# Products of a zero tile in every turn of an attention opening, and a new order at its end

## Chip, cores, metric

One core of a Trainium2 chip. The metric is the device time of one execution in microseconds; lower is better.

## The reference

Attention with a window and sinks, and two pairs of dense layers behind it:

```python
keep = (pos < n_sink) | ((rel >= 0) & (rel < window))      # n_sink 4, window 128, S = 768
a = softmax(where(keep, q @ k.T / 8, -1e9))                # B = 2, H = 8, D = 64
x = (a @ v) as [1536, 512]
h = x @ w_in;  g = max(h, 0) + alpha * min(h, 0);  y = g @ w_out       # 512 -> 2048 -> 512
h = y @ w2_in; g = h - tanh(h);                    out = g @ w2_out
```

## The kernel before

Queries and keys are divided into blocks of 128 positions: 12 units u (two batches of six blocks i), each with four pairs p of heads, so 48 pairs n = 4u + p. A pair goes through these steps, each on one engine:

- s_mm(n) (PE, lines 264 and 270): scores of the two heads of a pair, into two banks. In the opening these come from four banks "o", afterwards from "s" and "t". For the first unit the operands are the raw f32 tiles; later ones are split in a high and a low part by splits_hi (ACT, line 234) and splits_lo (DVE, line 237).
- s_max(n, a) (DVE, line 279): mask and row maximum; s_exp(n, a) (ACT, line 288): exponential and sum; norm_sum and norm (DVE, lines 294 to 303); sink_copy (DVE, line 309).
- t_mm(n) (PE, line 319): transposes into a bank "t" or "h", in turns; t_ev(n) (ACT, line 326) copies them out. sink_mm and sink_ev (PE line 341, ACT line 345) do the same for the sink columns; sink_mm(n - 1, n + 1) writes into the second score bank of pair n + 1.
- pv(n) (PE, lines 358 to 362): product with the values, line 362 for sinks; x_h (ACT, line 369) and x_l (DVE, line 374) copy a unit's sum out as a high and a low part.

The weights of the layers come as pairs of 32-bit words. A conversion makes them f32 in two ACT passes (lines 73 and 74, conv_start) and two DVE passes (lines 76 and 78, one conv_step each); load_w fetches a block of weights on SP's queue into one of two buffers, which the second DVE pass frees. split_w (ACT, line 215) and split_lo (DVE, line 220) then make high and low parts for the products, h_mm (line 389) and out_mm (line 441).

The kernel is written in the order in which each engine's queue runs it: nothing is reordered. The opening is a loop over S_LEAD = 19 turns n = 0 to 18. In turn n it issues the loads of the turn, s_mm(n + 1), t_ev(n - 2), s_max(n), s_exp(n), norm(n - 1), t_mm(n - 1), pv(n - 2), the splits of keys, and, by a table, conversions (0, 0) from turn 8 and (0, 1) from turn 12. After the loop conversion (0, 2) is started. Then 96 steps g follow, one for each block of 128 hidden units and 512 tokens, and the first 32 of them also carry the remaining pairs. Step 0 begins with t_mm(17), t_ev(17), sink_mm(17, 19) and sink_ev(17), and has s_mm(19) in the middle of its h_mm.

Of the kernel before, what the change touches and what calls it, by code (L numbers as in the profile page):

```python
# [14 lines left out]
BF16 = mybir.dt.bfloat16  # L15
# [7 lines left out]
S_LEAD = 19  # L23
CONV0 = ((0, 8), (1, 12))
# [7 lines left out]
CH = 512  # L32
# [106 lines left out]
def fast_path(tc, qk, v, vsink, limits, w1i, w1o, alpha, w2i, w2o, out, outer):  # L139
    nc = tc.nc  # L140
    keep = outer.enter_context(tc.tile_pool(name="keep", bufs=1))
    bad_i = keep.tile([1, 1], I32, name="bad_i")
    with ExitStack() as ctx:
        def pool(name, bufs=1, **kw):
            return ctx.enter_context(tc.tile_pool(name=name, bufs=bufs, **kw))
# [4 lines left out]
        gp = pool("g", 2)  # L150
# [49 lines left out]
        def conv_w(m, f):  # L200
            raw = stage[m][f % 2]
            if m == 1 and f < 3:
                wf[m, f] = ap.tile([128, 1024], F32, name="wf", tag="wx" if f == 2 else "pq", bufs=1 if f == 2 else 2)
            else:
                wf[m, f] = wp.tile([128, 1024], F32, name="wf", tag="wf", bufs=NF)
            at = m * NF + f
            yield from convert_scaled(nc, raw.rearrange("p (n t) -> p n t", t=2), wf[m, f], seen[:, at:at + 1])
# [3 lines left out]
        def split_w(m, c, f, part):  # L211
            src = wf[m, f][:, 512 * part:512 * part + 512]
            hi = wp.tile([128, 512], F32R, name=f"wh{part}", tag=f"wh{part}", bufs=2)
            lo = wp.tile([128, 512], F32R, name=f"wl{part}", tag=f"wl{part}", bufs=2)
            nc.scalar.activation(out=hi, in_=src, func=AF.Copy, scale=W_DOWN)  # L215
            whl[m, c, f, part] = (hi, lo)

        def split_lo(m, c, f, part):
            hi, lo = whl[m, c, f, part]
            nc.vector.scalar_tensor_tensor(lo, wf[m, f][:, 512 * part:512 * part + 512], W_DOWN, hi, op0=ALU.mult, op1=ALU.subtract)  # L220
# [3 lines left out]
        pq, sums, ptb, pts, vps, sks, sps, tps = {}, {}, {}, {}, {}, {}, {}, {}  # L224
        initial = [True]
# [19 lines left out]
        def ps_tile(tags):  # L245
            rot[0] += 1
            tag = tags[rot[0] % len(tags)]
            return ps.tile([128, 512], F32, name="ps_" + tag, tag=tag, bufs=4 if tag == "o" else 1)

        def geom(n):  # L250
            u, p = divmod(n, 4)
            b, i = divmod(u, NB)
            return u, p, b, i, (128 if i == 0 else 288)

        def s_mm(n):

            u, p, b, i, w = geom(n)
            for a in range(2):
                if (n, a) not in sps:
                    sps[n, a] = ps_tile(["o"] if initial[0] else ["st"[a]])  # L260
            if u == 0:
                for a in range(2):
                    t = raws[2 * u + p // 2][64 * a:64 * a + 64, p % 2]
                    nc.tensor.matmul(sps[n, a][:, :w], lhsT=t[:, 0, :], rhs=t[:, 1, :], start=True, stop=True)
                return
            at = 0 if u % 2 == 0 else K_ODD + 128
            for e, (l, r) in enumerate(((0, 0), (1, 0), (0, 1))):
                for a in range(2):
                    h = slice(64 * a, 64 * a + 64)
                    nc.tensor.matmul(sps[n, a][:, :w], lhsT=kq[l][h, p, at:at + 128], rhs=kq[r][h, p, K_EVEN:K_EVEN + w], start=e == 0, stop=e == 2)  # L270

        def s_max(n, a):
            u, p, b, i, w = geom(n)
            G, hh = 2 * u + p // 2, 2 * (p % 2) + a
            if hh == 0:
                pq[G] = ap.tile([128, 4, 288], F32, name="pq", bufs=2)
                sums[G] = ap.tile([128, 4], F32, name="sums", bufs=2)
            mask = m_zero if i == 0 else m_one if i == 1 else m_even if i % 2 == 0 else m_odd
            nc.vector.tensor_tensor_reduce(  # L279
                out=pq[G][:, hh, 0:w], in0=sps.pop((n, a))[:, :w], in1=mask[:, 0:w], scale=-0.125, scalar=BIG,  # L280
                op0=ALU.add, op1=ALU.min, accum_out=nm[:, 2 * n + a:2 * n + a + 1],
            )

        def s_exp(n, a):
            u, p, b, i, w = geom(n)
            G, hh = 2 * u + p // 2, 2 * (p % 2) + a
            e = pq[G][:, hh, 0:w]
            nc.scalar.activation(out=e, in_=e, func=AF.Exp, scale=-1.0, bias=nm[:, 2 * n + a:2 * n + a + 1], accum_out=sums[G][:, hh:hh + 1])  # L288
# [22 lines left out]
        def t_mm(n):  # L311
            u, p, b, i, w = geom(n)
            G, hh = 2 * u + p // 2, 2 * (p % 2)
            tps[n] = t = ps_tile(["t", "h"] if initial[0] else ["t"])
            cur = 0 if i % 2 == 0 else 160
            for a in range(2):
                for e, c in ((0, 160 - cur), (1, cur)):
                    if i > 0 or e == 1:
                        nc.tensor.transpose(t[:, 256 * a + 128 * e:256 * a + 128 * e + 128], pq[G][:, hh + a, c:c + 128], ident)  # L319

        def t_ev(n):
            u, p, b, i, w = geom(n)
            ptb[n] = ap.tile([128, 2, 2, 128], F32, name="pt", bufs=2)
            e0 = 1 if i == 0 else 0
            tv = tps.pop(n).rearrange("p (a e c) -> p a e c", a=2, e=2)
            nc.scalar.activation(out=ptb[n][:, :, e0:, :], in_=tv[:, :, e0:, :], func=AF.Copy)  # L326

        def has_sinks(n):
            u, p, b, i, w = geom(n)
            return p % 2 == 1 and i >= 2  # L330
# [12 lines left out]
        def sink_ev(n):  # L343
            pts[n // 2] = ap.tile([128, 128], F32, name="pts", bufs=2)
            nc.scalar.activation(out=pts[n // 2], in_=tps.pop((n, 0))[:, 384:512], func=AF.Copy)
# [142 lines left out]
        rel_i = wp.tile([128, 128], I32, name="rel_i", tag="wl0", bufs=2)  # L488
        rel = wp.tile([128, 128], F32, name="rel", tag="wh1", bufs=2)
        sink = wp.tile([128, 128], F32, name="sink", tag="wl1", bufs=2)  # L490
        nc.gpsimd.iota(rel_i, pattern=[[-1, 128]], base=0, channel_multiplier=1)
        nc.gpsimd.iota(col_i, pattern=[[1, 128]], base=0, channel_multiplier=0)
        make_identity(nc, ident)
# [26 lines left out]
        def a_loads(n):  # L520

            u, p = divmod(n, 4)
            if p == 3 and 2 <= u + 1 < NU:
                load_v(u + 1)
            if n % 2 == 0 and 6 <= n // 2 + 4 < 2 * NU:
                load_qk(n // 2 + 4)
            if n == 4 * NB + 4:
                load_vs(1)
# [19 lines left out]
        def conv_start(m, f):  # L548
            convs[m, f] = conv_w(m, f)
            next(convs[m, f])  # L550
# [5 lines left out]
        for n in range(S_LEAD):  # L556
            last = n == S_LEAD - 1
            a_loads(n)
            if n == 0:
                s_mm(0)  # L560
            if not last:
                s_mm(n + 1)
            if n >= 2:
                t_ev(n - 2)
            s_max(n, 0)
            s_max(n, 1)
            s_exp(n, 0)
            s_exp(n, 1)
            if n >= 2 and has_sinks(n - 2):
                sink_ev(n - 2)  # L570
            if n >= 1:
                norm_sum(n - 1, 0)
                norm_sum(n - 1, 1)
                norm(n - 1)
                sink_copy(n - 1)
                if not last:
                    t_mm(n - 1)
                    if has_sinks(n - 1):
                        sink_mm(n - 1, n + 1)
            if n >= 2 and not last:  # L580
                pv(n - 2)
            splits_hi(n)
            if n >= 5 and n % 4 == 1:
                x_h(n - 2)
            splits_lo(n)
            if n >= 5 and n % 4 == 2:
                x_l(n - 3)
            if n == 1:
                masks(0)
            if n == 4:  # L590
                masks(1)
            if n == 3:
                load_w(0, 1)
            for f, at in CONV0:
                if n == at:
                    conv_start(0, f)
                if at < n < at + 5:
                    conv_step(0, f)
                if n == at + 4:
                    load_w(0, f + 2)  # L600
                if n == at + 6 and f == 0:
                    split_w(0, 0, 0, 0)
                    split_lo(0, 0, 0, 0)
        initial[0] = False
        conv_start(0, len(CONV0))


        def flag():
# [36 lines left out]
        start = {t: f for f, t in enumerate(t for t in range(CONV1, CONV1 + NF + 1) if t != 2 * NF + 2)}  # L645
        for g in range(N):
            m, c, f = steps[g]
            n = S_LEAD + g
# [332 lines left out]
```

## Time and profile before

| | us |
|---|---|
| median of three runs | 668.03 (666.78 to 668.26) |
| the profiled execution | 665.62 |
| its span, first to last instruction | 663.9 |
| PE matmuls busy | 635.1 (96%) |
| DVE busy | 528.7 (80%) |
| ACT busy | 472.5 (71%) |

Busy time is that of instructions, without issues and semaphores. PE is the matmul part of TensorE, PEld its weight loads. A busy PE need not be at its peak: matmuls overlap, and the granted clock (PEclk, as a share of 2.4 GHz) has two levels.

### The profile page before, as it was taken

The numbers are of one execution on the slowest core, as the hardware profiler recorded it, in microseconds if no ns is written. First come the engines' busy times: TensorE is split into PE (matmuls) and PEld (weight loads), VectorE is DVE, ScalarE is ACT, GpSimd is POOL, SyncE is SP. The second block draws the span as 40 slices with busy tenths as digits, with TensorE's granted clock in tenths as the row PEclk, the third lists the DMA queues.
The fourth block names the chain that finished last, engine by engine and source line by source line (L and its number), as shares of the span: only waits on it lengthen the run. The fifth ranks groups of instructions, "written<-read, shape, count | busy, mean of one in ns | idle before, by whom it ended". The sixth has DMA issues, their size and how long they took to land.

```text
span 663.9 us, 9193 instructions
## 1 busy us (share of the span) xinstructions
PE 635.1 (96%) x3194; PEld 502.5 (76%) x3194; DVE 528.7 (80%) x1098; ACT 472.5 (71%) x936; POOL 1.1 (0%) x8
## 2 busy tenths in 40 slices
PE   5867999999999999999999999999999999999995
PEld 3545677777777777777888888888888888888884
DVE  7987888899576666548999978888898888888873
ACT  5877888787566565557877767777777777777763
POOL 0000000000000000000000000000000000000000
PEclk9988999999999999999999999999999999999999
DMA  5542444453010000214355500000010000100001
GB/s 157 190 147 95 144 159 173 165 202 112 3 46 17 1 16 1 77 53 170 147 190 191 190 1 1 0 1 0 1 64 0 2 0 1 63 1 1 0 1 69
DMA packets 27032, 47.36 MB, mean 71 GB/s; under 512 B 3168, under 2 KB 15456, under 8 KB 26976
## 3 DMA queue, kind: packets, MB, share of 16 engines
q1 hardware_dynamic: 26400, 46.42, 20.0%
q8 instruction: 27, 0.44, 0.3%
q10 hardware_dynamic: 576, 0.26, 0.2%
q14 instruction: 29, 0.24, 0.1%
HBM read 43.53 MB, written 3.15 MB: 70 GB/s over the span
## 4 chain that ended last, share of the span: by engine, by line
PE 82%; ACT 6%; DVE 6%; DMA 2%; issue 2%; SPq 0%; ACTq 0%; DVEq 0%
PE ps_o L441 36%; PE ps_h L389 19%; PE ps_s L389 9%; PE ps_t L389 8%; PE ps_s L270 2%; PE ps_t L319 2%; PE ps_v L358 2%; PE ps_v L362 2%; ACT wf L73 1%; PE ps_v L359 1%; DMA raw<-in_moe_w_out_dram 1%; DMA raw_qk<-in_qk_dram 1%; ACT raw L74 1%; DVE pq L279 1%; DVE wf L76 1%
## 5 line engine op out<-in xcount | busy, mean ns | idle before, releaser
L220 DVE SCALAR_TENSOR_TENSOR wl<-wf,wh 128x512 fp32r<-128x512 f32 x192 | 123.5, 683 | 44.1 <-ACT wh L215 44.1
L215 ACT ACTIVATE wh<-wf 128x512 fp32r<-128x512 f32 x192 | 110.8, 629 | 3.2 <-PE ps_o L441 3.1
L389 PE MATMUL ps_h<-x,wh 128*128 128x512 f32 x296 | 97.1, 409 | 0.3 <-DVE x L374 0.2
L441 PE MATMUL ps_o<-gh,wh 128*128 128x512 f32 x192 | 76.5, 398 | 0.0
L441 PE MATMUL ps_o<-wh,gh 128*128 128x512 f32 x192 | 74.8, 390 | 0.2 <-ACT gh L420 0.2
L441 PE MATMUL ps_o<-gh,wl 128*128 128x512 f32 x192 | 74.9, 390 | 0.0
L441 PE MATMUL ps_o<-wh,gl 128*128 128x512 f32 x192 | 74.8, 390 | 0.0
L441 PE MATMUL ps_o<-gl,wh 128*128 128x512 f32 x192 | 74.8, 390 | 0.0
L441 PE MATMUL ps_o<-wl,gh 128*128 128x512 f32 x192 | 74.7, 389 | 0.0
L288 ACT ACTIVATE pq<-pq,nm 128x288 f32<-128x288 f32 (+1 forms) x96 | 48.4, 506 | 30.3 <-DVE nm L279 29.8
L389 PEld LDWEIGHTS ps_h<-x,wh 128*128 128x128 f32 x296 | 52.5, 190 | 11.8 <-issue 2.0
L389 PE MATMUL ps_h<-x,wl 128*128 128x512 f32 x148 | 58.8, 397 | 0.3 <-DVE wl L220 0.3
L420 ACT ACTIVATE gh<-g 128x512 fp32r<-128x512 f32 x48 | 30.4, 633 | 29.6 <-DVE g L127 29.6
L326 ACT ACTIVATE pt<-ps_t 128x512 f32<-128x512 f32 (+1 forms) x39 | 21.9, 561 | 35.2 <-PE ps_t L319 35.1
L76 DVE SCALAR_TENSOR_TENSOR wf<-wf,raw 128x1024 int32<-128x1024 int32 x32 | 39.1, 1222 | 9.9 <-ACT raw L74 9.8
L441 PEld LDWEIGHTS ps_o<-gh,wh 128*128 128x128 f32 x192 | 36.0, 188 | 8.4 <-issue 1.4
L441 PEld LDWEIGHTS ps_o<-wh,gh 128*128 128x128 f32 x192 | 36.0, 188 | 8.0 <-ACT gh L420 0.6
L441 PEld LDWEIGHTS ps_o<-wh,gl 128*128 128x128 f32 x192 | 36.0, 188 | 7.9 <-DVE gl L425 0.4
L441 PEld LDWEIGHTS ps_o<-gh,wl 128*128 128x128 f32 x192 | 36.0, 188 | 7.7
L441 PEld LDWEIGHTS ps_o<-wl,gh 128*128 128x128 f32 x192 | 36.0, 188 | 7.5
L441 PEld LDWEIGHTS ps_o<-gl,wh 128*128 128x128 f32 x192 | 36.1, 188 | 7.1
L127 DVE COPY_PREDICATED g<-mask,t 128x512 f32<-128x512 int32 x48 | 36.4, 759 | 4.9
(155 smaller groups left out, 1339.4 us busy)
## 6 DMA issues: line engine op xcount, KB each, us to landing
raw<-in_moe_w_in_dram SPq DMA_DIRECT2D x32, 512.0 KB, 3.3
raw<-in_moe_w_out_dram SPq DMA_DIRECT2D x32, 512.0 KB, 4.2
raw_qk<-in_qk_dram SPq DMA_DIRECT2D x92, 64.0 KB, 3.0
vt<-in_v_dram SPq DMA_DIRECT2D x12, 256.0 KB, 3.2
out_dram<-ob SPq DMA_DIRECT2D x2, 1024.0 KB, 4.2
out_dram<-ob SPq DMA_DIRECT2D x4, 256.0 KB, 3.1
vs<-in_vsink_dram SPq DMA_DIRECT2D x2, 256.0 KB, 3.3
raw_qk<-in_qk_dram ACTq DMA_DIRECT2D x4, 64.0 KB, 2.8
```

The source lines that it names most:

```text
L76: nc.vector.scalar_tensor_tensor(di, di, 3, lw, op0=ALU.logical_shift_left, op1=ALU.bitwise_or)
L127: nc.vector.copy_predicated(g, mask.bitcast(I32), t)
L215: nc.scalar.activation(out=hi, in_=src, func=AF.Copy, scale=W_DOWN)
L220: nc.vector.scalar_tensor_tensor(lo, wf[m, f][:, 512 * part:512 * part + 512], W_DOWN, hi, op0=ALU.mult, op1=ALU.subtract)
L270: nc.tensor.matmul(sps[n, a][:, :w], lhsT=kq[l][h, p, at:at + 128], rhs=kq[r][h, p, K_EVEN:K_EVEN + w], start=e == 0, stop=e == 2)
L288: nc.scalar.activation(out=e, in_=e, func=AF.Exp, scale=-1.0, bias=nm[:, 2 * n + a:2 * n + a + 1], accum_out=sums[G][:, hh:hh + 1])
L319: nc.tensor.transpose(t[:, 256 * a + 128 * e:256 * a + 128 * e + 128], pq[G][:, hh + a, c:c + 128], ident)
L326: nc.scalar.activation(out=ptb[n][:, :, e0:, :], in_=tv[:, :, e0:, :], func=AF.Copy)
L358: nc.tensor.matmul(d, lhsT=vt[u - 1][:, h * D:(h + 1) * D], rhs=pt[:, a, 0, :], start=p == 0, stop=False)
L389: nc.tensor.matmul(h_ps[f], lhsT=l[:, w], rhs=x[:, r, kk, :], start=kk == 0 and e == 0, stop=kk == 3 and e == 2)
L420: nc.scalar.activation(out=gh, in_=mid[f], func=AF.Copy)
L441: nc.tensor.matmul(o, lhsT=l, rhs=r, start=f == 0 and e == 0, stop=f == NF - 1 and e == 2)
```

## The change

Five edits, all in the opening:

- A tile of 128 x 512 zeros in bf16 is made by POOL ahead of its other work. keep_busy(k, bank) multiplies it by itself k times into a bank; nobody reads the result.
- Nine such products stand at the start, before the first scores, in a bank "t".
- In every turn but the last, products follow s_mm(n + 1): four in turn 0, three in turn 1, eight in turn 2, two in each other. They go into the bank that t_mm(n - 1) of the same turn overwrites; that bank is now taken there, and t_mm uses it.
- load_w(0, 2) and load_w(0, 3) come one turn earlier (turns 11 and 15, not 12 and 16).
- split_w(0, 0, 0, 0) stays in turn 14, its split_lo moves from turn 14 to turn 16, and the start of conversion (0, 2) moves from behind the loop to the end of turn 16.

```diff
         def t_mm(n):
...
-            tps[n] = t = ps_tile(["t", "h"] if initial[0] else ["t"])
+            t = tps[n] if n in tps else ps_tile(["t"])
+            tps[n] = t
...
+        idle = gp.tile([128, CH], BF16, name="idle", tag="t", bufs=3)
+
+        def keep_busy(k, bank):
+            for _ in range(k):
+                nc.tensor.matmul(bank, lhsT=idle[:, 0:128], rhs=idle, start=True, stop=True)
+
+        nc.gpsimd.memset(idle, 0.0)
+        keep_busy(9, ps_tile(["t"]))
...
             if not last:
                 s_mm(n + 1)
+                tps[n - 1] = ps_tile(["t", "h"])
+                keep_busy({0: 4, 1: 3, 2: 8}.get(n, 2), tps[n - 1])
...
                     conv_step(0, f)
-                if n == at + 4:
+                if n == at + 3:
                     load_w(0, f + 2)
-                if n == at + 6 and f == 0:
-                    split_w(0, 0, 0, 0)
-                    split_lo(0, 0, 0, 0)
+            if n == S_LEAD - 5:
+                split_w(0, 0, 0, 0)
+            if n == S_LEAD - 3:
+                split_lo(0, 0, 0, 0)
+                conv_start(0, len(CONV0))
         initial[0] = False
-        conv_start(0, len(CONV0))
```

## Rows read from the trace of the kernel before

**Rows 1.** Stretches: its bounds and length, busy us (instructions) by engine, granted clock, DMA.
```profile
5.13:59.41 54.28, 41.98 (x298) 29.12 (x299) 46.04 (x187) 39.76 (x114) 0.00 (x0) 0.94 0.53 168
5.13:12.51 7.38, 4.43 (x18) 3.20 (x19) 5.54 (x31) 4.71 (x16) 0.00 (x0) 1.00 0.61 169
12.51:24.07 11.56, 11.56 (x62) 7.25 (x63) 10.85 (x52) 8.31 (x26) 0.00 (x0) 1.00 0.79 264
37.80:41.05 3.25, 3.25 (x18) 2.42 (x19) 1.84 (x8) 2.60 (x8) 0.00 (x0) 0.50 0.87 320
51.10:54.60 3.50, 3.50 (x20) 2.60 (x22) 2.61 (x11) 1.75 (x6) 0.00 (x0) 0.53 0.93 343
65.00:68.30 3.30, 3.30 (x14) 2.04 (x14) 3.20 (x11) 2.35 (x6) 0.00 (x0) 0.50 0.02 5
80.00:90.00 10.00, 10.00 (x59) 7.33 (x57) 9.61 (x20) 9.65 (x20) 0.00 (x0) 1.00 0.38 132
```

**Rows 2.** Timeline of PE: start, us, engine, line, instructions.
```profile
20.96 1.09 PE L270 MATMUL ps_o<-kq 64*128 64x288 f32 x6
...
25.85 0.66 PE L270 MATMUL ps_o<-kq 64*128 64x288 f32 x6
...
27.62 0.66 PE L270 MATMUL ps_o<-kq 64*128 64x288 f32 x6
```

**Rows 3.** Chain that ended last, in order of time: start, us, what.
```profile
64.57 2.50 PE ps_h L389 x6
...
83.19 1.39 PE ps_h L389 x6
...
86.77 2.72 PE ps_o L441 x12
```

**Rows 4.** Timeline of DVE; in brackets the idle time before, and its releaser.
```profile
21.71 0.69 DVE L374 TENSOR_TENSOR x<-ps_v,x 128x512 fp32r<-128x512 f32 x1 [0.30 <-ACT x L369]
...
29.73 1.23 DVE L76 SCALAR_TENSOR_TENSOR wf<-wf,raw 128x1024 int32<-128x1024 int32 x1 [0.78 <-ACT raw L74]
...
39.48 0.46 DVE L279 CUSTOM_DVE_ANT_0 pq<-ps_o,m_odd 128x288 f32<-128x288 f32 x1 [0.51 <-PE ps_o L270]
...
40.74 0.46 DVE L279 CUSTOM_DVE_ANT_0 pq<-ps_o,m_odd 128x288 f32<-128x288 f32 x1 [0.79 <-PE ps_o L341]
...
47.68 0.69 DVE L220 SCALAR_TENSOR_TENSOR wl<-wf,wh 128x512 fp32r<-128x512 f32 x1 [1.19 <-ACT wh L215]
...
49.43 0.45 DVE L279 CUSTOM_DVE_ANT_0 pq<-ps_o,m_odd 128x288 f32<-128x288 f32 x1
...
55.10 0.46 DVE L279 CUSTOM_DVE_ANT_0 pq<-ps_o,m_even 128x288 f32<-128x288 f32 x1 [1.29 <-PE ps_o L270]
```

**Rows 5.** Timeline of PE, instructions behind an idle time.
```profile
5.13 1.72 PE L264 MATMUL ps_o<-raw_qk 64*128 64x128 f32 x8 [5.13 <-DMA raw_qk<-in_qk_dram]
...
30.23 0.45 PE L358 MATMUL ps_v<-pt,vt 128*64 128x128 f32 x4 [1.37 <-ACT pt L326]
...
36.25 0.63 PE L319 MATMUL ps_h<-ident,pq 128*128 128x128 f32 x4 [1.75 <-DVE pq L303]
...
51.10 0.91 PE L319 MATMUL ps_h<-ident,pq 128*128 128x128 f32 x4 [3.64 <-DVE pq L303]
...
63.91 0.40 PE L270 MATMUL ps_s<-kq 64*128 64x288 f32 x1 [1.72 <-ACT pts L345]
```

**Rows 6.** Timeline of ACT, 58 to 68 us.
```profile
58.99 0.60 ACT L369 ACTIVATE x<-ps_v 128x512 fp32r<-128x512 f32 x1 [1.46 <-PE ps_v L362]
...
61.00 1.13 ACT L73 ACTIVATE wf<-raw 128x1024 f32<-128x1024 f32 x1
...
63.11 0.58 ACT L326 ACTIVATE pt<-ps_t 128x512 f32<-128x512 f32 x1
...
67.09 0.60 ACT L396 ACTIVATE t<-ps_h 128x512 f32<-128x512 f32 x1 [0.73 <-PE ps_h L389]
```

**Rows 7.** Timeline of POOL, start of the kernel.
```profile
1.20 0.28 POOL masks.py:197 MEMSET ident<- 128x128 f32 x1
```

## Prediction, made before the changed kernel ran

> **What bounds the kernel now.** I read the granted clock and the busy time by stretch first, then the chain that ended last, then what each engine waited for in the first 70 us. From about 80 us on, TensorE is the bound: a stretch of 10.00 us has 10.00 us of matmul [rows 1], and the chain of waits there is mostly products of the two layers [rows 3]. Nothing in the change touches that part, so I take it that an opening that ends earlier by some time brings the end forward by that time.
>
> The opening (turns n = 0 to 18, up to about 61 us) is another matter. From 5.13 to 59.41, PE is busy 41.98 of 54.28 us, DVE 46.04, ACT 39.76 [rows 1]. PE's figure is swollen by a low clock. The page prints a granted clock of 1.00 up to 37.80, but the same six score products take 1.09 us at 20.96 and 0.66 us at 25.85 [rows 2]: PE ran at the lower level, 1.2 GHz, until between these two. It fell back at 37.80, 51.10 and 65.00, each time for some 3.3 us [rows 1]. Ahead of the falls PE had sat idle 1.75 us (until 36.25), 3.64 us (until 51.10) and 1.72 us (until 63.91); no fall came after an idle of 1.37 us [rows 5]. The Trainium skill, "TensorE: Matmul & The Clock Gate", Part 1, says that the throttled level is the default and activity releases it, and warns that recorded clock events can be unreliable; both agree with these rows.
>
> The engine that sets the opening's pace is DVE. Where it does sit idle is to be seen one by one [rows 4]: 0.30 us at 21.71, 0.78 at 29.73, 0.51 and 0.79 at 39.48 and 40.74, 1.19 at 47.68, 1.29 at 55.10. A gain in the opening has to come out of these, or out of the ACT queue behind 61.00, where DVE and PE wait together.
>
> **The change part by part.**
>
> *The zero products.* Each is 512 columns wide. I cost one by the 512-column products here: 2.50/6 = 0.42 us at the low clock, 2.72/12 = 0.23 us at the full one [rows 3]. They are in bf16, which the trace lacks; those rows are the bound above, and 0 (PE idle anyway) the one below. There are 9 before turn 0, then 4, 3 and 8, then 2 in each of turns 3 to 17: 54, or 12.3 us at the full clock. In a turn they stand behind s_mm(n+1) and ahead of t_mm(n-1). Their bank is the one that t_ev(n-3) empties, and pv(n-3), a turn earlier on PE, has waited for that already: no new wait. Queued behind them are t_mm, sink_mm and pv; t_mm waits for DVE's norm in any case, so they are free where PE is early.
>
> *The start.* POOL first clears the zero tile. Its 128x128 f32 memset takes 0.28 us [rows 7]; this tile has twice the bytes and four times the elements, so 0.56 to 1.12 us; begun where POOL's first work of the kernel begins, 0.4 us before that memset's 1.20, it is ready at 1.4 to 1.95. Nine products at 0.42 end at 5.2 to 5.75, while the first score products now start at 5.13 [rows 5]. Loss 0.1 to 0.6 us; I take 0.3, nearer the lower end since a rise within the nine shortens them. POOL's iotas come later too, but DVE does nothing with them that is urgent before the limits land. PE then works without a break: nine products (3.8 us), the eight of s_mm(0) and s_mm(1) (1.72 us, [rows 5]) and four more (1.7 us), to about 9 us. So I expect the rise there and not near 24.
>
> *5 to 31 us.* With the full clock, PE is no longer late for x_h: the 0.30 us of DVE at 21.71 goes. ACT waited there too; ahead of L74 it then runs about 1 us earlier, and most of the 0.78 at 29.73 goes. Gain 1.0 of 1.08; below, 0, if ACT is held by DVE in the old places.
>
> *37.8 to 41 us.* The idle of 1.75 us before 36.25 gets two products (0.45), leaving 1.3, less than the 1.37 that was followed by no fall. If the clock stays, s_mm(13) ends by 38.75 and the 0.51 goes; two products push t_mm(11) and sink_mm back by 0.45, so of the 0.79 only a little goes. s_max(13, 1) starts near 40.1 instead of 40.74 [rows 4]: gain 0.6 (0 if the clock falls, 1.1 if the products hide).
>
> *split_lo moved from turn 14 to 16.* DVE now waits 1.19 us, until 47.68, for ACT's split_w, and then takes about 0.6 for split_lo; both leave turn 14, and L78 follows x_l directly. s_max(15) starts at 47.6 instead of 49.43 [rows 4]: 1.8 us earlier. In turn 16 the 0.61 falls where DVE idles 1.29 us [rows 4], so it stays hidden there; without that cover the gain would be 1.2. The long PE idle before 51.10 shortens by the same 1.8, and by 0.45 of products, to about 1.4.
>
> *Turns 16 and 17.* Now t_mm(14) starts 1.67 us behind s_max(15) (51.10 to 49.43, [rows 4, 5]); then at 49.3. A PE turn without idle is 27.62 - 25.85 = 1.77 us [rows 2], and pv(13) has about 0.7 of sink products, so s_mm(17) ends at 51.7, two products at 52.15, t_mm(15) and sink_mm at 53.0. DVE, through s_max(16), norm(15), sink_copy and the moved split_lo, comes to s_max(17, 0) at 52.5 instead of 55.10: 2.6 us earlier, of which 1.8 are counted and 0.8 are new, nearly all of it the low clock from 51.10 on. Its second half waits for the sink_mm at 53.0; 0 if the clock falls again.
>
> *conv_start(0, 2) moved from behind turn 18 to turn 16.* On ACT it fills 61.00 to 63.11, and t_ev(17) behind it, at 63.11, empties the t bank (sink_ev behind it the s bank): PE waits 1.72 us until 63.91 [rows 5, 6]. In turn 16 it goes behind kq_hi, 52.3 to 54.5, and makes t_ev(15) and s_exp(17) late; but ACT idles 1.46 us before 58.99 [rows 6], which pays most of it. s_exp(18) then ends at 59.1 and t_ev(17) starts there: 4.0 us earlier than 63.11, of which 2.6 are counted. Gain 1.4 (bounds: 2.1 if all is hidden, 0 if pv(15) and x_h behind t_ev(15) come late).
>
> *Behind 60 us.* With no PE idle of 1.72 us the fall at 65.00 should go. Six hidden products then take 1.39 instead of 2.50 us [rows 3], but the copy out of them (67.09, [rows 6]) stands behind s_exp(19) on ACT, at 62.8: 4.3 earlier in all, 0.3 new.
>
> *The loads a turn earlier.* load_w(0, 2) and load_w(0, 3) leave when the conversions (0, 0) and (0, 1) have freed their buffers. In SP's queue they come to stand ahead of load_qk(10) and load_qk(12) instead of behind them, so those keys now wait for the conversions too. The keys are first read in turns 16 and 21, four turns or more behind their place in the queue, and conversion (0, 2) reads its weights at 52 us, so I cost both at nothing. Without that cover a late key would hold s_mm, and all of DVE behind it, for one turn (about 2 us).
>
> **Sum:** +0.3 - 1.0 - 0.6 - 1.8 - 0.8 - 1.4 - 0.3 = -5.6 us. The profiled execution took 665.62 us (span 663.9 and 1.7 around it), so 660.0 for one like it. The runs shown have a median of 668.03, 2.4 above it; from there 662.4. A measurement tells about 0.2% (1.3 us) from no change.
>
> **The rivals.**
>
> *The products hold PE back (664 to 666.0).* With 0.45 of products a PE turn of 1.77 becomes 2.2 us, and turns 10 to 17 add sink products. If the 0.45 stands on the path in all eight, 3.6 of the 5.6 go: 666.0. For it: in turns 12 and 16 my own walk has PE late. Against: 41.98 us of PE work, less about half of the low-clock stretches (11.56 + 3.25 + 3.50 and part of 4.43, [rows 1]: about -10), plus 12.3, is 44 of 54 us. The Trainium skill, same page, Part 2, says that matmuls stay in program order and only weight loads are pulled ahead. By that no transpose overtakes a zero product; were all 30 of turns 3 to 17 on the path, that is 6.8 us, 669.2.
>
> *The clock falls in spite of them (664.1).* The idles left, 1.3 and 1.4 us, lie close to the 1.72 that was followed by a fall. Then the terms 0.6, 0.8 and 0.3 go: 5.6 - 1.7 = 3.9, 664.1.
>
> *Zero products don't raise the clock (slower, 670.9).* Then 25 of them in turns 0 to 7 cost 0.42 each, 10.5 us; PE's idle of 7.38 - 4.43 = 2.95 in 5.13 to 12.51 [rows 1] hides some and 7.5 stay; the 1.0 is not won, and of the gains 4.9 are left (5.9 less 1.0): +0.3 + 7.5 - 4.9 = +2.9. It decides if the low clock lasts past about turn 6, at 0.84 us a turn. Against it: the rise near 24 came behind short real products alone [rows 1], and PE is no less occupied by zeros.
>
> *Given back later (668.0).* What comes earlier out of the opening could wait the longer behind 61 us, for weights or ACT. Against: PE is full from 80 us on [rows 1], and loads there start when a conversion frees a buffer, so they come earlier with the rest.
>
> **Chances.** Forecast 0.60 (own range 660.0 to 664.0); products on the path 0.14; falls 0.12; not raised 0.07; given back 0.07. Range 659.8 to 666.4: it takes in the second and third cases, and a gain of 8 us if the ordinary runs lose more to low clock than the profiled one did. Faster: the first three, less 0.04 for their weak ends, 0.82; same 0.10; slower 0.08.
>
> **What would show it.** Right: score products at 0.66 us by turn 3; no granted clock of 0.50 between 24 and 70 us; no DVE wait at L220 in turn 14; conversion (0, 2) on ACT before 56 us; the first s_mm into the s and t banks near 60 instead of 63.91; the first matmul of scores at 5.2 to 5.75. Wrong: t_mm waiting for PE rather than for DVE in most turns, a fall near 36 or 48 us, or scores still at 1.09 us at 15 us.

## The result and the profile after

| | before | changed |
|---|---|---|
| median, us | 667.40 (four runs, 666.58 to 668.26) | 659.89 (four runs, 659.62 to 660.14) |
| profiled execution | 665.62 | 660.14 |
| its span | 663.9 | 658.4 |

The ratio of the times is 0.9897, with an interval of 0.9879 to 0.9915: some 6.9 us faster. The forecast was 662.4 (659.8 to 666.4); the measured median lies 0.1 us above the lower end of that range. Between the two profiled executions the gain is 5.48 us, where the sum of the terms said 5.6.

The clock first. These are the windows of the changed kernel, with the columns of [rows 1]:

```profile
5.28:57.00 51.72, 44.39 (x345) 26.91 (x349) 46.39 (x189) 42.88 (x120) 0.00 (x0) 1.00 0.56 181
12.51:24.07 11.56, 10.87 (x82) 5.95 (x85) 11.21 (x53) 9.28 (x29) 0.00 (x0) 1.00 0.80 268
37.80:41.05 3.25, 3.20 (x30) 2.19 (x30) 2.66 (x12) 3.24 (x7) 0.00 (x0) 1.00 0.63 191
60.00:70.00 10.00, 8.84 (x56) 6.26 (x55) 9.04 (x21) 9.63 (x21) 0.00 (x0) 1.00 0.38 132
```

From the first scores on, no stretch of the opening has a low clock any more. PE has 44.39 us of work in it, close to the 44 that the prediction worked out, and DVE still has more, 46.39. The products and the first scores, in the timelines of POOL and PE:

```profile
0.75 0.53 POOL L498 MEMSET idle<- 128x512 bf16 x1 [0.29 <-POOLq L980]
...
1.33 4.02 PE L496 MATMUL ps_t<-idle 128*128 128x512 bf16 x9 [1.33 <-POOL idle L498]
5.28 1.14 PE L264 MATMUL ps_o<-raw_qk 64*128 64x128 f32 x8
...
13.11 0.66 PE L270 MATMUL ps_o<-kq 64*128 64x288 f32 x6
```

The nine products take 0.45 us each, and right behind them the eight products of the first scores take 1.14 us instead of 1.72 [rows 5]. So the clock rose at about 5.3 us, as the first real product began; the same six score products that took 1.09 us at 20.96 [rows 2] take 0.66 at 13.11.

Next, the places at which engines waited before, now in the timelines of DVE, of PE and of ACT:

```profile
29.30 1.23 DVE L76 SCALAR_TENSOR_TENSOR wf<-wf,raw 128x1024 int32<-128x1024 int32 x1 [1.17 <-ACT raw L74]
...
39.40 0.46 DVE L279 CUSTOM_DVE_ANT_0 pq<-ps_o,m_odd 128x288 f32<-128x288 f32 x1 [0.48 <-PE ps_o L342]
...
50.49 0.68 DVE L220 SCALAR_TENSOR_TENSOR wl<-wf,wh 128x512 fp32r<-128x512 f32 x1
51.09 0.45 DVE L279 CUSTOM_DVE_ANT_0 pq<-ps_o,m_even 128x288 f32<-128x288 f32 x1
```

```profile
29.80 0.45 PE L359 MATMUL ps_v<-pt,vt 128*64 128x128 f32 x4 [1.33 <-ACT pt L327]
...
35.73 0.72 PE L320 MATMUL ps_h<-ident,pq 128*128 128x128 f32 x4 [1.10 <-DVE pq L303]
...
47.77 0.72 PE L320 MATMUL ps_h<-ident,pq 128*128 128x128 f32 x4 [0.91 <-DVE pq L303]
...
58.56 0.40 PE L270 MATMUL ps_s<-kq 64*128 64x288 f32 x1
```

```profile
26.50 0.63 ACT L234 ACTIVATE kq<-raw_qk 128x512 fp32r<-128x512 f32 x1 [0.79 <-DMA raw_qk<-in_qk_dram]
...
50.76 1.17 ACT L73 ACTIVATE wf<-raw 128x1024 f32<-128x1024 f32 x1
...
57.54 0.59 ACT L327 ACTIVATE pt<-ps_t 128x512 f32<-128x512 f32 x1
...
61.33 0.57 ACT L397 ACTIVATE t<-ps_h 128x512 f32<-128x512 f32 x1
```

Lines of the pairs' functions and behind are one higher than before (t_mm is now L320). The reader is to see three things. The 1.19 us wait at L220 is gone (50.49, in turn 16, no idle in front), and so is the wait of 1.29 in front of s_max(17, 0). PE's idles of 1.75 and 3.64 us [rows 5] are now 1.10 and 0.91, and the 1.72 us in front of the first s_mm behind the loop are gone (58.56). And one wait has grown: DVE's 0.78 us in front of L76 [rows 4] is now 1.17, because ACT stood 0.79 us waiting for a load of keys at 26.50.

The gain, read off at the points that the prediction's steps name (each point's start, before and after, and the difference):

| point | before | after | gain so far | this step | forecast of it |
|---|---|---|---|---|---|
| first splits_lo (L237) | 7.84 | 7.61 | 0.23 | 0.2 | -0.3 |
| s_max(10, 0) | 30.87 | 30.44 | 0.43 | 0.2 | 1.0 |
| s_max(13, 1) | 40.74 | 39.40 | 1.34 | 0.9 | 0.6 |
| s_max(15, 0) | 49.43 | 46.19 | 3.24 | 1.9 | 1.8 |
| s_max(17, 0) | 55.10 | 51.09 | 4.01 | 0.8 | 0.8 |
| t_ev(17) | 63.11 | 57.54 | 5.57 | 1.6 | 1.4 |
| copy out of h (L396, now L397) | 67.09 | 61.33 | 5.76 | 0.2 | 0.3 |

I then followed the copies of the first layer's result (gh), step by step through the 96 steps. They are 5.80 us earlier from 73 to 87 us, 5.40 at 96, 5.06 at 103, 5.38 at 111, and stay between 5.3 and 5.5 nearly all the way to the end, 5.43. So 0.4 of the gain is lost once, near 83 us.

### The profile page after: what moved, and what is told of

Same layout as the page of the kernel before. It is cut to its first block, busy times and chain, and to the rows that moved or that the text cites. A ratio compares the mean times of both kernels' runs of the same rounds, so it can differ in the third digit from the quotient of the medians.

```text
span 658.4 us, 9283 instructions
## 1 busy us (share of the span) xinstructions
PE 639.4 (97%) x3243; PEld 500.0 (76%) x3248; DVE 528.2 (80%) x1098; ACT 472.0 (72%) x936; POOL 1.7 (0%) x9
## 4 chain that ended last, share of the span: by engine, by line
PE 79%; DVE 10%; ACT 5%; DMA 3%; issue 2%; SPq 0%; DVEq 0%; ACTq 0%
PE ps_o L442 36%; PE ps_h L390 19%; PE ps_s L390 9%; PE ps_t L390 8%; PE ps_s L270 2%; DVE pq L279 2%; DMA raw_qk<-in_qk_dram 1%; DMA raw<-in_moe_w_out_dram 1%; PE ps_t L320 1%; PE ps_v L359 1%; DVE wf L78 1%; PE ps_v L363 1%; DVE wf L76 1%; ACT raw L74 1%; DVE wl L220 1%
## 5 line engine op out<-in xcount | busy, mean ns | idle before, releaser
L220 DVE SCALAR_TENSOR_TENSOR wl<-wf,wh 128x512 fp32r<-128x512 f32 x192 | 123.5, 683 | 42.9 <-ACT wh L215 42.9
L442 PE MATMUL ps_o<-gh,wl 128*128 128x512 f32 x192 | 74.9, 390 | 0.0
L76 DVE SCALAR_TENSOR_TENSOR wf<-wf,raw 128x1024 int32<-128x1024 int32 x32 | 39.1, 1223 | 8.6 <-ACT raw L74 8.2
```

Of the source, the lines that this page charges most:

```text
L76: nc.vector.scalar_tensor_tensor(di, di, 3, lw, op0=ALU.logical_shift_left, op1=ALU.bitwise_or)
L442: nc.tensor.matmul(o, lhsT=l, rhs=r, start=f == 0 and e == 0, stop=f == NF - 1 and e == 2)
```

## The experiments

In each, the edit is to the changed kernel. All ratios are to the kernel before, run on the same chip as the experiment, with an interval of 95%.

### The two halves of the change

**The order without the products.** No zero tile, t_mm takes its bank itself; the loads, split_lo and the conversion stand in the new order.

```diff
-            t = tps[n] if n in tps else ps_tile(["t"])
-            tps[n] = t
+            tps[n] = t = ps_tile(["t", "h"] if initial[0] else ["t"])
...
-        nc.gpsimd.memset(idle, 0.0)
-        keep_busy(9, ps_tile(["t"]))
...
-                tps[n - 1] = ps_tile(["t", "h"])
-                keep_busy({0: 4, 1: 3, 2: 8}.get(n, 2), tps[n - 1])
```

> The new order without any zero product. Theory (about half of the gain is order, half is clock): split_lo's wait of 1.19 us and the conversion behind turn 18 are gone, about 3.3 us of the 7.5 us between the medians, so near 664 us, with granted clock 0.50 still seen near 38 and 51 us and scores at 1.09 us until past 20 us. Rival A (the order is all, low clock was hidden behind DVE and ACT): within 1 us of the changed kernel, 659.5 to 661. Rival B (the clock is all): 666 to 667.4.

Measured: 662.06 us (661.13 to 663.88), ratio 0.9935 (0.9911 to 0.9959), profiled 661.92. The order alone brings some 4.3 us, more than expected. Its timeline of PE and two windows:

```profile
36.79 0.63 PE L319 MATMUL ps_h<-ident,pq 128*128 128x128 f32 x4 [1.74 <-DVE pq L303]
...
48.53 0.70 PE L319 MATMUL ps_h<-ident,pq 128*128 128x128 f32 x4 [1.63 <-DVE pq L303]
```

```profile
36.80:40.20 3.40, 3.40 (x33) 2.59 (x35) 3.20 (x14) 2.79 (x8) 0.00 (x0) 1.00 0.95 349
49.00:52.30 3.30, 3.30 (x20) 2.40 (x18) 2.75 (x11) 1.95 (x9) 0.00 (x0) 0.50 0.92 337
```

An idle of 1.74 us was followed by no fall of the clock here, and one of 1.63 us by the only fall of this run's opening.

**The products without the order.**

```diff
-                if n == at + 3:
+                if n == at + 4:
                     load_w(0, f + 2)
-            if n == S_LEAD - 5:
-                split_w(0, 0, 0, 0)
-            if n == S_LEAD - 3:
-                split_lo(0, 0, 0, 0)
-                conv_start(0, len(CONV0))
+                if n == at + 6 and f == 0:
+                    split_w(0, 0, 0, 0)
+                    split_lo(0, 0, 0, 0)
         initial[0] = False
+        conv_start(0, len(CONV0))
```

> The old order with all 54 zero products. Theory: the clock part alone, some 4 us, so near 663.5; DVE waits 1.2 us at split_lo in turn 14 again and PE waits for the conversion behind turn 18. Rival A (order is all): 666 to 668. Rival B (clock is all): 659.5 to 661.

Measured: 665.72 us (664.97 to 666.71), ratio 0.9988 (0.9977 to 0.9998), profiled 665.68. The products alone bring some 0.8 us between runs and nothing between the profiled executions, less than the 4 us expected. Together the two bring 6.9 where the parts add up to 5.1, and 5.5 against 3.6 in the profiled executions (3.7 and -0.1). Why the whole is more than its parts shows in this run's timelines, of DVE and of PE, and its window behind them:

```profile
46.25 0.69 DVE L220 SCALAR_TENSOR_TENSOR wl<-wf,wh 128x512 fp32r<-128x512 f32 x1 [1.50 <-ACT wh L215]
...
54.79 0.46 DVE L279 CUSTOM_DVE_ANT_0 pq<-ps_o,m_even 128x288 f32<-128x288 f32 x1 [1.39 <-PE ps_o L342]
```

```profile
49.58 0.72 PE L320 MATMUL ps_h<-ident,pq 128*128 128x128 f32 x4 [3.14 <-DVE pq L303]
```

```profile
50.00:55.00 5.00, 5.00 (x34) 3.52 (x34) 2.95 (x13) 2.52 (x7) 0.00 (x0) 0.66 0.62 222
```

In the old order DVE waits for split_w with the pairs' work behind it, PE sits idle for 3.14 us in spite of the two products ahead of that, and the clock falls. What DVE had gained it gives back in waits for scores (1.39 at 54.79).

Only part of the difference in the profiled executions arises there. By the copies of gh at 73 us this run is 1.25 us ahead of the kernel before, the order alone 3.78 and the changed kernel 5.81, so in the opening the whole exceeds its parts by 0.8 us. This run then loses 0.4 us near 87, and 0.9 at 307.5, where ACT waits 3.12 us for weights (2.23 in the kernel before).

**The first 24 products alone, and the other 30 alone.**

```diff
-                keep_busy({0: 4, 1: 3, 2: 8}.get(n, 2), tps[n - 1])
+                keep_busy({0: 4, 1: 3, 2: 8}.get(n, 0), tps[n - 1])
```

> New order, the 24 products of the start and turns 0 to 2, none in turns 3 to 17. Theory (the early rise matters, the two per turn hold the clock): PE's idle times of 1.33, 1.10 and 0.91 us grow to 1.8, 1.5 and 1.4, a fall comes back in some place near 35 us, time 660.5 to 661.5. Rival (the two per turn cost time on PE's path and the clock stays without them): 658.5 to 659.5.

```diff
-        keep_busy(9, ps_tile(["t"]))
+        ps_tile(["t"])
...
-                keep_busy({0: 4, 1: 3, 2: 8}.get(n, 2), tps[n - 1])
+                keep_busy(0 if n < 3 else 2, tps[n - 1])
```

> New order, two products in each of turns 3 to 17, none at the start and in turns 0 to 2. Theory: the clock stays low until past 15 us, and ten products at 0.42 us in turns 3 to 7 then stand on PE's path: 662 to 664. Rival (DVE hides the low clock and the products): 659.5 to 661.

Measured: with the first 24 alone 662.16 us (661.32 to 663.12), ratio 0.9936 (0.9919 to 0.9954), the same as the order without any product. With the other 30 alone, against the 662 to 664 expected, 660.58 us (659.84 to 661.27), ratio 0.9911 (0.9894 to 0.9928), and a profiled span of 658.1, shorter than the changed kernel's 658.4. So nearly all that the products are worth lies in the two of each later turn. The windows of the run with the first 24 alone:

```profile
12.51:19.50 6.99, 4.83 (x41) 3.10 (x40) 6.78 (x35) 5.40 (x18) 0.00 (x0) 1.00 0.85 259
19.70:22.90 3.20, 3.14 (x20) 2.16 (x22) 3.10 (x15) 2.63 (x8) 0.00 (x0) 0.50 0.92 333
36.70:39.90 3.20, 3.20 (x16) 2.52 (x15) 1.86 (x9) 2.36 (x7) 0.00 (x0) 0.50 0.81 271
50.40:53.60 3.20, 3.20 (x20) 2.39 (x19) 2.57 (x11) 2.82 (x7) 0.00 (x0) 0.50 0.65 214
```

The clock, up since the start, falls three times. Ahead of the last two falls PE had idled 1.74 and 1.75 us (until 35.48 and 48.64). Ahead of the first it had no long idle at all; its timeline up to that fall:

```profile
14.68 0.43 PE L320 MATMUL ps_h<-ident,pq 128*128 128x128 f32 x2 [0.65 <-DVE pq L303]
...
16.84 0.43 PE L320 MATMUL ps_t<-ident,pq 128*128 128x128 f32 x2 [0.76 <-DVE pq L303]
...
18.99 0.63 PE L320 MATMUL ps_h<-ident,pq 128*128 128x128 f32 x4 [0.75 <-DVE pq L303]
```

Three idles of 0.65 to 0.76 us close to each other were followed by a fall. At the full clock, and without the two products a turn, PE is too quick for DVE here. Between 12.51 and 19.50, up to the fall, this run's PE worked 4.83 of 6.99 us; the changed kernel's worked 6.49:

```profile
12.51:19.50 6.99, 6.49 (x49) 3.48 (x49) 6.78 (x35) 5.13 (x17) 0.00 (x0) 1.00 0.82 260
```

### Two of the order's edits, undone one at a time

The third, the two loads a turn earlier, was not undone by itself.

**split_lo back in turn 14.**

```diff
-            if n == S_LEAD - 5:
-                split_w(0, 0, 0, 0)
+                if n == at + 6 and f == 0:
+                    split_w(0, 0, 0, 0)
+                    split_lo(0, 0, 0, 0)
             if n == S_LEAD - 3:
-                split_lo(0, 0, 0, 0)
                 conv_start(0, len(CONV0))
```

> The changed kernel with split_w and split_lo of (0, 0, 0, 0) put back into their old place in turn 14. Theory: DVE waits 1.2 to 1.5 us for split_w there; the 0.6 of split_lo itself leaves turn 16, where it was partly hidden, so 1.2 to 1.9 us slower: 661.1 to 661.8, more if PE's idle time of over 3 us lets the clock fall. Rival (the wait was caused by the low clock, not by the order): equal within 0.3 us and no wait at L220.

Measured: 663.92 us (663.13 to 664.95), ratio 0.9962 (0.9951 to 0.9973); the profiled span is 3.7 us longer than the changed kernel's. Its timelines of DVE and PE and a window:

```profile
46.24 0.69 DVE L220 SCALAR_TENSOR_TENSOR wl<-wf,wh 128x512 fp32r<-128x512 f32 x1 [1.50 <-ACT wh L215]
...
53.94 0.46 DVE L279 CUSTOM_DVE_ANT_0 pq<-ps_o,m_even 128x288 f32<-128x288 f32 x1 [1.57 <-PE ps_o L270]
```

```profile
49.56 1.11 PE L320 MATMUL ps_h<-ident,pq 128*128 128x128 f32 x4 [3.14 <-DVE pq L303]
```

```profile
48.20:54.50 6.30, 4.94 (x24) 3.48 (x25) 4.46 (x20) 3.73 (x12) 0.00 (x0) 0.50 0.68 229
```

The move is worth twice its own 1.9 us. The rest goes with the clock: with the wait of 1.50 us at L220 back, the products can't hold it, and it stays at 1.2 GHz for over six microseconds, with DVE waiting 1.57 us for scores at the end of them.

**Conversion (0, 2) back behind the loop.**

```diff
-                conv_start(0, len(CONV0))
         initial[0] = False
+        conv_start(0, len(CONV0))
```

> The changed kernel with the start of conversion (0, 2) put back behind turn 18, all else as changed. Theory: ACT passes of 2.1 us stand ahead of t_ev(17) again, PE waits for the s and t banks, 1.4 to 1.7 us slower: 661.3 to 661.6; PE idles over 1.5 us there, so a fall of the clock may add up to 1 us. Rival (ACT's new waits in turns 16 and 17 had cost as much as the move won): equal within 0.3 us.

Measured: 661.80 us (661.40 to 662.86), ratio 0.9927 (0.9912 to 0.9943); the span is 2.7 us longer. One row of PE says why:

```profile
59.71 0.42 PE L270 MATMUL ps_s<-kq 64*128 64x288 f32 x1 [1.83 <-ACT pts L346]
```

PE's idle at the first s_mm of the second phase is back (1.83 us, before 1.72), a fall follows it from 59.9 to 63.4 us, and the copy out of h starts at 63.51 instead of 61.33: 2.2 us, of which 1.4 are there by the start of t_ev(17) (58.89 instead of 57.54). The other 0.5 us of the span lie behind the last copy of gh.

### Where the missing part of the first term went

**load_w(0, 1) three turns later.** In the changed kernel this load is issued at 17.64 us and the keys that ACT waits for at 26.50 stand behind it on SP's queue (issued from 19.61 on).

```diff
-            if n == 3:
+            if n == 6:
                 load_w(0, 1)
```

> The changed kernel with load_w(0, 1) in turn 6 instead of turn 3, so behind load_qk(6) and load_qk(7) on SP's queue. Theory (the gain of the first 30 us was lost at ACT's wait of 0.79 us for raw_qk at 26.50, behind that megabyte of weights): the wait goes, DVE's 1.17 us before the first L76 shrinks to 0.4 or less, the time falls by 0.6 to 0.9 us below the changed kernel's 659.9 (659.0 to 659.3). Rival (DVE's pace holds ACT there anyway): the same time as the changed kernel within 0.3 us, with DVE still idle about 1.1 us.

Measured: 660.79 us (659.70 to 661.31), ratio 0.9909 (0.9892 to 0.9927), no gain over the changed kernel where 0.6 to 0.9 was expected. In its trace ACT's wait for the keys is gone and DVE's in front of L76 falls from 1.17 to 0.33:

```profile
28.89 1.23 DVE L76 SCALAR_TENSOR_TENSOR wf<-wf,raw 128x1024 int32<-128x1024 int32 x1 [0.33 <-ACT raw L74]
```

From 73 to 87 us this run is 6.20 us ahead of the kernel before, 0.4 more than the changed kernel; at 96 us it is 5.42 ahead. So the late keys cost about 0.4 us of the opening in the trace of the changed kernel, and something behind it takes that back.

That the order on the queue makes the keys late is not shown by this. The run with split_lo back in turn 14 issues load_w(0, 1) in its old place, ahead of the keys, and differs from the changed kernel only from turn 14 on. ACT doesn't wait for keys in it either, and its DVE waits as little:

```profile
28.89 1.22 DVE L76 SCALAR_TENSOR_TENSOR wf<-wf,raw 128x1024 int32<-128x1024 int32 x1 [0.33 <-ACT raw L74]
```

The changed kernel once more (below) has a wait for keys of 0.54 us at the same place. So the wait comes in some executions and not in others with the same queue; what decides it stays open.

**The same, without the first 24 products.** Both edits, of this run and of that with the other 30 alone.

> As the run before, but without the 24 products of the start and turns 0 to 2. Theory (an early rise of the clock is worth something only where the keys are there in time): 0.5 to 1.0 us slower than the run with the 24 products, 659.8 to 660.3. Rival (the low clock of the first 20 us is hidden behind DVE whatever the loads do): equal to it within 0.3 us.

Measured: 660.06 us (659.08 to 660.41), ratio 0.9898 (0.9879 to 0.9917). At 73 us it is 5.22 ahead of the kernel before, 1.0 behind the last run, as expected of the first products; but it keeps the 5.22 to the end, where the last run has 5.61. So in the traces the first 24 products are worth about 1.0 us in the opening when the keys are not late, and 0.4 of it at the end; the medians, 660.06 without them and 660.79 with them, go the other way.

### The loss near 83 us, and how many products are right

The changed kernel's chain of waits shows the place (start, us, what):

```profile
77.62 5.48 DMA raw<-in_moe_w_out_dram
...
83.18 1.25 ACT wf L73 x2
```

The weights of load_w(0, 5) land 5.48 us after their issue, and ACT waits 1.07 us for them. In the runs that lose nothing here the same load lands in 4.0 to 4.8 us. In the records of the DMA queues the two kinds of run differ in a fetch of 16 KB of instructions (TensorE's, to go by how it moves with the number of products). Where it starts 0.35 to 0.56 us ahead of the issue of the weights, at 77.1 us in the changed kernel, they land late. Products of the zero tile are instructions too, so their number moves the fetch. Three runs and the changed kernel once more tested that.

**The changed kernel once more**, with no edit:

> The changed kernel once more, on the same chip as the next three. Time 659.6 to 660.8. Theory of the loss near 83 us: a fetch of instructions of 16 KB starts near 77.3 us, in the middle of the weight load issued at 77.2 to 77.6, that load lands 5.5 us after its issue instead of 4.2, and ACT waits about 1.1 us for it. Rival (that landing was chance): no such wait this time.

**Three products instead of two in turns 3 to 10**, and the same with load_w(0, 1) in turn 6:

```diff
-                keep_busy({0: 4, 1: 3, 2: 8}.get(n, 2), tps[n - 1])
+                keep_busy({0: 4, 1: 3, 2: 8}.get(n, 3 if n <= 10 else 2), tps[n - 1])
```

> The changed kernel with three instead of two products in turns 3 to 10: eight products more, 16 instructions more on TensorE's queue. Theory: by the 5.0 us that 24 products less had moved it, the fetch moves some 1.7 us earlier, to about 75.6, between two weight loads; the load issued near 77 lands in 4.2 us, ACT does not wait, and the 0.4 us lost between 87 and 96 us is not lost: 0.3 to 0.5 us faster than the changed kernel if the products are hidden. Rival (the products are on PE's path): 0.5 to 1.8 us slower.

> As the run before, with load_w(0, 1) in turn 6. Theory: both losses are gone (0.4 us at raw_qk near 26 us, 0.4 to 0.8 us at the weights near 83 us): span near 657.5 in the profiled execution, and 0.7 to 1.2 us faster than the changed kernel in the medians. Rival (other transfers take the place of those): no faster than the changed kernel, with a new wait for a transfer between 20 and 100 us.

**Four products instead of two in turns 3 to 17:**

```diff
-                keep_busy({0: 4, 1: 3, 2: 8}.get(n, 2), tps[n - 1])
+                keep_busy({0: 4, 1: 3, 2: 8}.get(n, 4), tps[n - 1])
```

> The changed kernel with four products instead of two in each of turns 3 to 17. Thirty products more, 6.8 us of PE. Theory: PE's idle times in the opening (0.2 to 1.3 us in front of six instructions) take some; turns 9 to 17 have PE late at sink_mm already, so two thirds stand on the path there: 2 to 4 us slower, 662 to 664. Rival (DVE sets the pace throughout): within 0.5 us of the changed kernel. Rival 2 (all on the path): 666 or more.

Measured, all on one chip:

| run | median, us | ratio | span | fetch at | ahead at 73 us | at 96 us | at the end |
|---|---|---|---|---|---|---|---|
| changed again | 660.61 | 0.9907 (0.9887 to 0.9927) | 658.8 | 77.1 | 5.99 | 5.32 | 5.3 |
| three to turn 10 | 659.77 | 0.9899 (0.9879 to 0.9920) | 657.6 | 74.3 | 6.33 | 6.34 | 6.4 |
| three, load later | 659.70 | 0.9888 (0.9866 to 0.9910) | 658.9 | 74.9 | 6.09 | 5.75 | 5.6 |
| four each | 660.61 | 0.9908 (0.9888 to 0.9928) | 658.3 | 74.6 | 5.48 | 5.49 | 5.6 |

The issue of those weights, in the timeline of SP's queue, and the window of the last 0.75 us before they land: first the changed kernel, then the run with three products to turn 10.

```profile
77.62 0.73 SPq L198 DMA_DIRECT2D raw<-in_moe_w_out_dram  x1
```

```profile
82.35:83.10 0.75, 0.75 (x5) 0.61 (x4) 0.75 (x2) 0.00 (x0) 0.00 (x0) 1.00 0.19 55
```

```profile
77.09 0.43 SPq L198 DMA_DIRECT2D raw<-in_moe_w_out_dram  x1
```

```profile
80.77:81.52 0.75, 0.75 (x5) 0.63 (x4) 0.75 (x2) 0.75 (x2) 0.00 (x0) 1.00 1.01 296
```

With the fetch at 76.7 to 77.1 (the changed kernel, the same once more, and the run with load_w(0, 1) later) even the issue takes longer, 0.73 to 1.30 us against 0.43, and these three lose 0.4, 0.7 and 0.8 us between 73 and 96. The DMA share, 0.19 against 1.01 at the end of the load, says that most of the sixteen engines have finished while a few are still at it.

Three of the experiments above show the same, with everything later: the products without the order, conversion (0, 2) back, and split_lo back. There the fetch starts at 81.7, 79.3 and 80.7 us, 0.4 to 0.5 ahead of the issue, which takes 0.80 to 0.99; the weights land in 5.4 to 5.6 us, and 0.4 to 0.5 us are lost.

In the runs where the fetch starts elsewhere (74.3, 74.6, and 82.1 and 82.5 in the two runs without the first products) nothing is lost there. The one that loses 0.3 with the fetch at 74.9 has another late load: issued at 62.52, it landed in 5.40 us with no fetch near it. So not every late landing is the fetch.

Three products to turn 10 give the shortest profiled span, 657.6, and a median 0.8 us below the changed kernel's on the same chip; the intervals overlap, so it can't be told from it. Its version with the later load is no better in its profile.

Four products each answer a rival. I had expected the 30 more to cost 2 to 4 us, and the medians are the same, 660.61 in both. A window, two rows of PE and one of DVE of that run:

```profile
5.28:57.00 51.72, 48.55 (x371) 30.09 (x377) 46.19 (x189) 42.56 (x119) 0.00 (x0) 1.00 0.59 180
```

```profile
35.46 0.72 PE L320 MATMUL ps_h<-ident,pq 128*128 128x128 f32 x4 [0.68 <-DVE pq L303]
...
47.95 0.72 PE L320 MATMUL ps_h<-ident,pq 128*128 128x128 f32 x4 [0.32 <-DVE pq L303]
```

```profile
39.57 0.46 DVE L279 CUSTOM_DVE_ANT_0 pq<-ps_o,m_odd 128x288 f32<-128x288 f32 x1 [0.93 <-PE ps_o L342]
```

PE's work grows by 4.16 us in that stretch and DVE's stays the same (46.19, 46.39); the idles of 1.10 and 0.91 us shrink to 0.68 and 0.32. So most of the price of a product is idle time of PE. It is not all of it: DVE's wait for sink_mm at 39.57 is 0.93 us, 0.48 in the changed kernel, and at 73 us this run is 5.48 ahead of the kernel before, where the changed kernel's two traces are 5.81 and 5.99 ahead. The 0.3 to 0.5 us that the 30 products cost there are made up near 83 us, where this run loses nothing.

## Why the prediction was right

**What bounds the opening.** DVE was named as its pace. The run with four products each bears it out: 48.55 us of matmuls in 51.72, and the opening only 0.3 to 0.5 us longer. The rival in which the products stand on the path (664 to 666.0, or 669.2) fell with it, though a small part of that price is there.

**The start (+0.3).** Off by 0.5 the other way. The memset took 0.53 us, under the range that I gave it, and the nine products end at 5.35, the early end of 5.2 to 5.75. But I had the clock rise at about 9 us; it rose at 5.3, so that the first scores took 1.14 instead of 1.72 us. The prediction's second paragraph took the 1.00 that is printed near the start for a wrong record. It is a gap and not an error: the first record of the clock in each trace is its rise, at 24.00 us in the kernel before and at 5.30 here, and the windows print 1.00 for all that lies ahead of it. So they do over the nine products, though these took 0.45 us each and later ones 0.24.

**5 to 31 us (-1.0).** This term was mis-sized: -0.2. The clock was up and x_h no longer late, as I said; but ACT, early, ran into keys that had not landed, 0.79 us. I had walked the queue for the loads that the diff moves, and not for those that it leaves in place while their reader comes earlier. In two traces where ACT finds the keys there (load_w(0, 1) later, and split_lo back) DVE's 1.17 us become 0.33 and s_max(10, 0) starts at 30.03 instead of 30.44; as the second has the queue of the changed kernel, what makes the keys late stays open.

**37.8 to 41 (-0.6), split_lo (-1.8), turns 16 and 17 (-0.8), conversion (0, 2) (-1.4), behind 60 (-0.3).** Measured 0.9, 1.9, 0.8, 1.6 and 0.2: right, each within 0.3. The first was larger since of DVE's waits of 0.51 and 0.79 us only 0.48 is left.

**The sum and the median.** 5.6 against 5.48 in the profiled executions, with the first two errors (0.5 better, 0.8 worse), the small ones of the other terms (0.5 better in all) and the 0.4 lost near 83 us cancelling: that the sum is so close is luck. That an earlier end of the opening is carried through whole was so but for that 0.4; the rival in which all is given back is refuted. From there I added 2.4 us, the distance between the profiled execution of the kernel before and its median, and that was wrong: the changed kernel's runs lie at 659.62 to 660.14, its profiled execution among them. Part of the 2.4 us was chance: in the three later series of the kernel before, on three chips, the medians are 666.39 to 666.95, only 0.8 to 1.3 above that execution. Part goes with the clock. Of those 36 runs 30 had a mean granted clock of 0.988 to 0.991, as the profiled one (0.991), and took 664.87 to 667.62 us; six had 0.983 to 0.985 and took 667.66 to 669.41. All ten runs of the changed kernel had 0.996 to 0.999. So some executions of before lose more to the low clock than the one in the trace, and the change takes that away too. Of the four runs that the result compares with, two (668.03, 668.26) lie where those six lie; their clock is not on record. I had this case as the lower end of the range and not as the forecast, and the median came out nearly there. Where in those executions the further falls lie no trace shows.

**The clock in the changed kernel.** The rival in which it falls all the same did not come about here, but it lay close: it is what happens with either of the two halves missing. The order alone leaves PE idles of 1.74 and 1.63 us in front of 36.79 and 48.53, and a fall at 49.0; the products alone leave 3.14 us, and a fall at 51.0. The order shortens PE's wait, and the products fill what is left of it. The Trainium skill, "TensorE: Matmul & The Clock Gate", Part 1, section "HAM oscillation — how this bites in real kernels", describes a kernel whose PE is throttled anew in each wait for a transfer; this trace agrees in kind, with a wait for another engine in the transfer's place. What the prediction had wrong about it is the sign that it looked for. It compared the longest single idle (no fall after 1.37, falls after 1.72). The fall at 19.6 in the run with the first 24 alone came after idles of at most 0.76 us; the changed kernel has one of 1.33 without a fall, and the order alone one of 1.74. The idles have to be seen together with the work between them; what sum of the two decides no run here shows.

**That zero products don't raise the clock.** Refuted by the row at 5.28.

**Still open.** That the instruction fetch makes the weights land late rests on the runs in which it moved, in both directions, on the longer issue in all six traces that have it just ahead of the issue, and on the DMA share at the end of the load; no run moved the fetch alone. The Trainium skill, "DMA: Bandwidth & Descriptors", section "Queues, rings and completion order", says that a DMA engine changes from one queue to another only between whole packets. A fetch that is one packet of 0.93 us in the changed kernel (1.42 in the run with load_w(0, 1) later) would hold up one of the sixteen engines for somewhat less than these two loads are late, an estimated 1.2 and 1.6 us (5.48 and 5.88 less the 4.3 of the run with the other 30 products alone); no run here shows which engine it was, nor why the issue takes longer.

## What to carry to other kernels

A stretch whose pace another engine sets can have room on TensorE for products that nobody reads, and these can hold its clock up; how many is not critical (four a turn gave the same time as two here, and cost 0.3 to 0.5 us of the opening) as long as TensorE still waits for the other engine. But look for long waits first: products that fill part of a wait of over 3 us did not hold the clock, and the move that shortened the wait was worth twice its own time once they were there. And where a stage is made earlier, walk the queues for the transfers that are left in place: here late keys and late weights took 0.4 us each in the trace of the changed kernel, some of what an earlier opening had won.

## What the runs showed of the hardware

- The clock fell after three idles of TensorE of 0.65 to 0.76 us, each some 2 us behind the one before, with 4.83 us of matmuls in the 6.99 us up to the fall; it did not fall in the changed kernel with 6.49 in the same 6.99.
- The longest single idle does not tell whether the clock falls: it did not after 1.33 us (changed kernel) and 1.74 us (the order alone), and it did after 1.63 us (the order alone), 1.72 and 1.75 us (kernel before).
- A fetch of 16 KB of instructions that starts 0.35 to 0.56 us ahead of the issue of a 512 KB load goes with a longer issue (0.73 to 1.30 us instead of 0.43) and a later landing (5.4 to 5.9 us instead of 4.0 to 4.8), in six traces. Eight more products in the opening moved it from 77.1 to 74.3 us.
- The six runs of the kernel before with a mean granted clock of 0.983 to 0.985 are slower than all 30 with 0.988 to 0.991; among the 30, 664.87 to 667.62 us, the clock does not explain the spread. With the clock held up in the opening the changed kernel's four runs lie within 0.5 us, and its six later ones within 1.5.
